# Two halves of a transposed tile in two PSUM pools instead of one

## The chip, the cores and the metric

The kernel runs on one core of a Trainium2 chip. The metric is the device time of one execution in microseconds (us).

## The reference

An adaLN block: modulation vectors come from a condition `c`; then grouped-query attention with cached K and V (32 query heads, 8 KV heads, 2048 queries, 2048 keys, head size 128), then a gMLP block.

```python
mod = (_silu(c) @ w_mod).reshape(c.shape[0], 6, 1, -1)
sa, ca, ga, sb, cb, gb = ...
h = _layernorm(x) * (1 + ca) + sa
x = x + ga * attention(h)          # q = h @ wq; softmax(q k^T / sqrt(128)) v; @ wo
h = _layernorm(x) * (1 + cb) + sb
x = x + gb * gmlp(h)
```

The part that matters is how the first 512 rows of `h` reach the query projection: the kernel normalises a tile of 128 rows, transposes it on PE (TensorE) into PSUM, where this kernel's matmuls and transposes put their results, lets VectorE apply the modulation on the way to SBUF (`hT`), and projects.

## The kernel before

The kernel takes PSUM in tiles of 512 f32 columns, which it calls banks: two score tiles `s_ps` of two banks each, two banks `misc` and two banks `o_ps`. Each name has its own rotation of two; a request gets the bank of the request before last under the same name, and the first write must wait until that earlier tile has been read.

```python
psum = fast.enter_context(tc.tile_pool(name="psum", bufs=2, space=bass.MemoryType.PSUM))
def bank(name):
    return psum.tile([P, 512], FP32, name=name)
def bank2():
    return psum.tile([P, 1024], FP32, name="s_ps")
...
def ln1_turn(j0, n, xns):
    ch, c0 = j0 // CT, (j0 % CT) * P
    hT = hT_of(ch)
    for half in range(2):
        t_ps = bank("misc")[:].bitcast(BF16).rearrange("p (k q) -> p k q", k=2)
        for k in range(2):
            dt = half * 2 + k
            for jj in range(n):
                nc.tensor.transpose(t_ps[:, k, jj * P : (jj + 1) * P],
                                    xns[jj][:, dt * P : (dt + 1) * P], ident[:])   # L827
        for k in range(2):
            dt = half * 2 + k
            dst, src = hT[:, dt, c0 : c0 + n * P], t_ps[:, k, 0 : n * P]
            ln1_mod(dst, src, dt)                                                  # L809, VectorE
```

The query projection takes a `misc` bank, too, and empties it with a VectorE cast:

```python
def qproj(b, heads, c0, n):
    ...
        if dt == 0 and (not one or hh == heads[0]):
            ps[0] = bank("misc")
        ... nc.tensor.matmul(ps[0][...], lhsT=wqs[g][...], rhs=hTs[ch][...])       # L940
            nc.vector.tensor_copy(out=dst, in_=src)                                # L951
```

The attention is cut into units (one query tile and one KV group) of eight slots. "Scores (u, i)" below are the two QK matmuls of unit u, slot i (L973), followed by ScalarE's exponential (L980); "P·V" are the eight matmuls of a slot that use the exponentials of the unit before (L995). In the first unit there is no P·V yet, and the turns and projections of tiles 1 to 3 are put between its scores:

```python
at(0, 3, first_turn)                              # ln1_turn(1, 1), ahead of scores (0,3)
at(0, 6, lambda: ln1_turn(2, 2, first["x2"]))     # tiles 2 and 3, ahead of scores (0,6)
fill[0, 0] = [first_norm]
for i in (1, 2, 3):
    fill[0, i] = [lambda: warm(1)]                # a matmul into o_ps that nobody reads (L781)
next_q = qproj(0, list(range(REP)), P, P)         # projection of tile 1
fill[0, 4], fill[0, 5] = next_q[0:8], next_q[8:16]
rest_q = qproj(0, [0, 1], 2 * P, 2 * P) + qproj(0, [2, 3], 2 * P, 2 * P)
fill[0, 7] = rest_q[0:4]                          # behind scores (0,7)
```

## Time and profile before

| | before |
|---|---|
| time, median of 3 runs | 1321.55 us (1321.16 to 1321.85) |
| span of the profiled run | 1320.0 us |
| PE busy | 1311.8 us (99%) |
| ScalarE busy | 1077.1 us (82%) |
| scores (0,0) start | 10.65 us |
| scores (2,0) start | 27.31 us |
| last PE matmul ends | 1313.68 + 0.84 = 1314.52 us |

In the timeline, a line gives the start and the length of a group of like instructions, the engine (PE is TensorE, DVE VectorE, ACT ScalarE), the source line, the operation, and the tiles out<-in with their shapes; brackets give idle time ahead of it and what ended it. A group's length runs from its first start to its last end, and the ends of matmuls are modelled; so I measure by starts. The prediction shows the groups around the wait in question. Two more lines of the timeline of PE in the kernel before are needed below as marks, the starts of scores (0,0) and (2,0), and one for the end:

```profile
10.65 0.59 PE L973 MATMUL s_ps<-qT,kT 128*128 128x512 bf16 x2
...
27.31 0.60 PE L973 MATMUL s_ps<-qT,kT 128*128 128x512 bf16 x2
...
1313.68 0.84 PE L1357 MATMUL s_ps<-wout_sb,yT 128*128 128x512 bf16 x2
```

From the first of these to the second it is 16.66 us. This distance, taken inside one trace, is free of what happens ahead of the first scores, and it is what the experiments compare.

### The profile page before, as it was taken

How to read it: one execution, taken by the hardware profiler on the slowest of the kernel's cores; microseconds unless marked ns; L12 is line 12 of the kernel's file. 1: busy time of each engine (PE TensorE's matmuls, PEld its weight loads, DVE VectorE, ACT ScalarE, POOL GpSimd, SP SyncE). 2: the span in 40 equal slices, each digit the busy share in tenths (PEclk: the TensorE clock that was granted, in tenths of full speed). 3: DMA queues.
4: the chain of work that ended last, by engine and by line, in shares of the span. 5: the costliest groups of instructions: out<-in, count | busy, mean ns of one | idle time of the engine just before them, and what ended most of it. 6: DMA issues, size and time to landing. Idle time of an engine off the chain costs nothing.

```text
span 1320.0 us, 27930 instructions
## 1 busy us (share of the span) xinstructions
PE 1311.8 (99%) x12359; PEld 857.8 (65%) x12359; DVE 471.7 (36%) x1162; ACT 1077.1 (82%) x1061; POOL 51.8 (4%) x96
## 2 busy tenths in 40 slices
PE   9999999999999999999999999999999999999998
PEld 5666666666666666666666666666666666644445
DVE  5622222222222222222222222222222566794444
ACT  7899999999999999999999999999999999650000
POOL 1201000000000000000000000000000000020000
PEclk9999999999999999999999999999999999999999
DMA  7542121112101111211111211121111112143300
GB/s 180 141 104 47 20 45 37 37 17 50 37 17 37 30 37 37 33 33 38 33 37 13 53 38 33 18 53 22 32 14 21 25 31 33 33 112 84 69 21 26
DMA packets 148944, 58.64 MB, mean 44 GB/s; under 512 B 138480, under 2 KB 144880, under 8 KB 148816
## 3 DMA queue, kind: packets, MB, share of 16 engines
q1 hardware_dynamic: 141792, 37.65, 15.6%
q0 software_dynamic: 4432, 16.91, 4.5%
q8 instruction: 98, 1.61, 0.5%
q10 hardware_dynamic: 2592, 2.23, 0.5%
q14 instruction: 30, 0.25, 0.1%
HBM read 21.89 MB, written 2.10 MB: 18 GB/s over the span
## 4 chain that ended last, share of the span: by engine, by line
PE 99%; DMA 0%; DVE 0%; ACT 0%; SPq 0%; issue 0%; DVEq 0%
PE o_ps L995 35%; PE s_ps L973 34%; PE misc L1027 8%; PE misc L940 8%; PE misc L1336 7%; PE s_ps L1182 2%; PE s_ps L1221 2%; PE o_ps L1357 1%; PE s_ps L1357 1%; DMA wmod_a<-in_w_mod_dram 0%; PE misc L850 0%; ACT pT L980 0%; PE misc L1344 0%; PE o_ps L781 0%; PE misc L827 0%; DVE qT L951 0%
## 5 line engine op out<-in xcount | busy, mean ns | idle before, releaser
L980 ACT ACTIVATE pT<-s_ps 128x1024 bf16<-128x1024 f32 x1024 | 1043.8, 1024 | 82.5 <-PE s_ps L973 7.4
L995 PEld LDWEIGHTS <-pT 128*128 128x128 bf16 x8192 | 548.2, 98 | 241.5
L995 PE MATMUL o_ps<-v,pT 128*128 128x129 bf16 x8192 | 631.7, 220 | 0.0
L973 PE MATMUL s_ps<-qT,kT 128*128 128x512 bf16 x2048 | 609.1, 379 | 0.6 <-ACT pT L980 0.5
L1006 DVE RECIPROCAL rall<-o_ps 128x2 f32<-128x2 f32 x256 | 43.7, 171 | 742.9 <-PE o_ps L995 739.5
L973 PEld LDWEIGHTS <-kT 128*128 128x128 bf16 x2048 | 199.0, 98 | 119.6 <-issue 1.0
L1027 PE MATMUL misc<-wo_g,oT 128*128 128x512 bf16 x512 | 194.2, 379 | 0.0
L940 PE MATMUL misc<-hT,wq_g 128*128 128x512 bf16 (+2 forms) x528 | 190.3, 371 | 0.0
L1007 DVE TENSOR_TENSOR onorm<-o_ps,rall 128x256 bf16<-128x256 f32 x256 | 108.7, 425 | 8.8
L1336 PE MATMUL misc<-wsp,z 128*128 128x512 bf16 (+2 forms) x560 | 100.7, 337 | 0.0
L951 DVE CAST qT<-misc 128x512 bf16<-128x512 f32 x127 | 86.4, 681 | 3.1 <-PE misc L940 3.1
L1336 PEld LDWEIGHTS <-z 128*128 128x128 bf16 x560 | 50.5, 98 | 48.5
L1040 DVE TENSOR_TENSOR xacc<-misc,xacc 128x512 f32<-128x512 f32 x112 | 76.2, 680 | 0.0
L940 PEld LDWEIGHTS <-wq_g 128*128 128x128 bf16 x528 | 50.4, 98 | 0.8
L1027 PEld LDWEIGHTS <-oT 128*128 128x128 bf16 x512 | 50.0, 98 | 0.9
L1351 DVE TENSOR_TENSOR gb<-misc,bsp_bc 128x512 bf16<-128x512 f32 (+1 forms) x28 | 18.4, 658 | 58.5 <-PE misc L1336 58.5
L1182 PE MATMUL s_ps<-win_sb,hT 128*128 128x448 bf16 x128 | 27.0, 353 | 0.0
L1192 ACT ACTIVATE z<-s_ps 128x896 bf16<-128x896 f32 x16 | 14.7, 917 | 14.9 <-PE s_ps L1182 14.9
L1221 PE MATMUL s_ps<-hT,win_sb 128*128 128x512 bf16 x112 | 24.5, 379 | 0.0
L1229 ACT ACTIVATE z1T<-s_ps 128x1024 bf16<-128x1024 f32 x14 | 14.3, 1024 | 10.1 <-PE s_ps L1221 9.1
L692 DVE BATCH_NORM_STATS2 bnst<-x_sb 128x6 f32<-128x512 bf16 x32 | 21.9, 683 | 1.3 <-DMA x_sb<-in_A_x_dram 0.8
L1357 PE MATMUL o_ps<-wout_sb,yT 128*128 128x512 bf16 x84 | 20.1, 379 | 0.0
(86 smaller groups left out, 268.9 us busy)
## 6 DMA issues: line engine op xcount, KB each, us to landing
wq_g<-in_A_wq_dram POOLq DMA_DIRECT2D x7, 512.0 KB, 3.9
v<-in_A_v_cache_dram POOLq DMA_DIRECT2D x7, 512.0 KB, 5.8
wo_g<-in_A_wo_dram POOLq DMA_DIRECT2D x7, 512.0 KB, 4.7
oT<-onorm SPq DMA_TRANSPOSE x128, 2.4
wsp<-in_w_mod_dram POOLq DMA_DIRECT2D x1, 2048.0 KB, 11.8
out_dram<-yout ACTq DMA_DIRECT2D x16, 128.0 KB, 1.7
win_sb<-in_B_w_in_dram POOLq DMA_DIRECT2D x1, 1792.0 KB, 7.7
x_sb<-in_A_x_dram SPq DMA_DIRECT2D x3, 512.0 KB, 5.6
```

Source lines behind the costliest of these rows:

```text
L940: nc.tensor.matmul(ps[0][:, o0 : o0 + n], lhsT=wqs[g][:, dt, hh * DH : (hh + 1) * DH], rhs=hTs[ch][:, dt, c0 : c0 + n], start=(dt == 0), s ...
L951: nc.vector.tensor_copy(out=dst, in_=src)
L973: nc.tensor.matmul(s_ps[:, h * 512 : (h + 1) * 512].rearrange("p (r q) -> p r q", r=REP), lhsT=groups[g]["kT"][:, kt * P : (kt + 1) * P], ...
L980: nc.scalar.activation(out=pTs[u][:, 2 * i : 2 * i + 2, :], in_=s_ps[:].rearrange("p (k q) -> p k q", k=2), func=ACT.Exp, scale=inv_sqrt_dh,)
L995: nc.tensor.matmul(o_ps[:, hh % 2, 0 : DH + 1], lhsT=pTs[u][:, kt, hh * P : (hh + 1) * P], rhs=groups[g]["v1"][:, kt, 0 : DH + 1], start=( ...
L1007: nc.vector.tensor_tensor(out=onorms[u][:, hh - 1 : hh + 1, :], in0=o_ps[:, :, 0:DH], in1=rall[:, c0 : c0 + 2].unsqueeze(2).to_broadcast([ ...
L1027: nc.tensor.matmul(X_ps[:], lhsT=oTs[u][:, hh, :], rhs=groups[g]["wo"][:, hh, :], start=(hh == 0), stop=(hh == REP - 1),)
L1040: nc.vector.tensor_tensor(out=xaccs[j][:], in0=X_ps[:], in1=xaccs[j][:], op=ALU.add)
L1182: nc.tensor.matmul(ps[0][:, hf * 512 : hf * 512 + FC], lhsT=h2Ts[j // CT][:, dt, (j % CT) * P : (j % CT + 1) * P], rhs=win_sb[:, dt, FH + ...
L1221: nc.tensor.matmul(ps[0][:, k * 512 : (k + 1) * 512], lhsT=win_sb[:, dt, f * P : (f + 1) * P], rhs=h2Ts[2 * ch2 + k][:, dt, :], start=(dt ...
L1336: nc.tensor.matmul(g_ps[:, :n], lhsT=z2[:, st, f * P : (f + 1) * P], rhs=wsp[t][:, st, c0 : c0 + n], start=(st == 0), stop=(st == NT - 1 a ...
L1357: nc.tensor.matmul(dst, lhsT=yT[:, f, jj * P : (jj + 1) * P], rhs=wout_sb[:, f, :], start=(f == 0), stop=(f == NFT - 1),)
```

## The change

The second half of a turn is to get its PSUM bank from another pool, so that the two halves don't queue in the rotation of `misc`.

```diff
@@ ln1_turn
         for half in range(2):
-            t_ps = bank("misc")[:].bitcast(BF16).rearrange("p (k q) -> p k q", k=2)
+            t_ps = bank(("misc", "o_ps")[half])[:].bitcast(BF16).rearrange("p (k q) -> p k q", k=2)
             for k in range(2):
```

## The prediction

> **What bounds the kernel now.** I read the page first: the shares of the engines and the chain that ended last.
>
> ```profile
> span 1320.0 us, 27930 instructions
> PE 1311.8 (99%) x12359; PEld 857.8 (65%) x12359; DVE 471.7 (36%) x1162; ACT 1077.1 (82%) x1061; POOL 51.8 (4%) x96
> ...
> PE 99%; DMA 0%; DVE 0%; ACT 0%; SPq 0%; issue 0%; DVEq 0%
> ```
>
> PE is busy for 1311.8 of 1320.0 us and is 99% of the chain of waits. So a microsecond counts only if PE's own stream gets it: PE runs in program order, and what it loses near the start moves everything behind it. The changed lines belong to the first pass over the queries, so the next view is who PE waited for, over the whole run:
>
> ```profile
> PE o_ps L781 <- DVE onorm L763: 1.2, 1, 1.2
> PE misc L827 <- DVE qT L951: 0.6, 1, 0.6
> PE s_ps L973 <- ACT pT L980: 0.5, 2, 0.2
> PE misc L850 <- DMA wmod_a<-in_w_mod_dram: 0.2, 1, 0.2
> ```
>
> The second line is the one that the change is about: L827 is the PE transpose in the changed function, and it waited once, 0.6 us, for a VectorE cast. The timeline of PE around it (columns: start, length, engine, line, operation, tiles, then in brackets idle time and what ended it):
>
> ```profile
> 15.61 0.61 PE L940 MATMUL misc<-hT,wq_g 128*128 128x128 bf16 x8
> 16.05 0.39 PE L827 MATMUL misc<-ident,xn 128*128 128x128 bf16 x4
> 17.00 0.39 PE L827 MATMUL misc<-ident,xn 128*128 128x128 bf16 x4 [0.56 <-DVE qT L951]
> 17.22 1.03 PE L973 MATMUL s_ps<-qT,kT 128*128 128x512 bf16 x4
> 18.08 0.60 PE L940 MATMUL misc<-hT,wq_g 128*128 128x256 bf16 x4
> 18.93 0.59 PE L973 MATMUL s_ps<-qT,kT 128*128 128x512 bf16 x2 [0.24 <-ACT pT L980]
> ```
>
> and of VectorE and ScalarE:
>
> ```profile
> 16.25 0.69 DVE L951 CAST qT<-misc 128x512 bf16<-128x512 f32 x1 [0.51 <-PE misc L940]
> 16.86 1.36 DVE L809 TENSOR_SCALAR hT<-misc,modc 128x256 bf16<-128x256 bf16 x4
> 18.14 0.68 DVE L692 BATCH_NORM_STATS2 bnst<-x_sb 128x6 f32<-128x512 bf16 x1
> ...
> 17.85 1.02 ACT L980 ACTIVATE pT<-s_ps 128x1024 bf16<-128x1024 f32 x1 [0.97 <-PE s_ps L973]
> ```
>
> The misc pool has two buffers, handed out in turn. Counting in the source: the first query projection (L940, ended at about 16.2) holds one, the first half of the turn of tiles 2 and 3 (16.05) gets the other, and the second half needs the first one again, which the cast at 16.25 must empty. The cast ends at 16.94 and PE goes on at 17.00. The score matmuls (L973) stand behind these transposes, so ScalarE's exponential starts at 17.85 after 0.97 us idle.
>
> **What the Trainium skill says.** "Perfetto Trace Analysis", section Matmuls: "Independent matmul groups should rotate through different PSUM banks so the ACT/DVE evacuation of one overlaps the next group's matmuls". The trace shows what happens when the rotation is one bank short: the 0.56 us above. "PSUM — Partial Sum Buffer", section Engine vs sequencer instructions: matmuls start and complete in program order. The trace agrees: the scores at 17.22 follow the held transposes by one issue step. The same page, section PSUM bank collisions raise a hardware error, says that the chip neither arbitrates nor stalls, so that a bank must be guarded by semaphores; hence the wait is the price of the shared bank and can be removed only by another bank. No run here shows a collision.
>
> **The change part by part.** The function is called twice: for one tile (transposes at 13.10) and for two (16.05 and 17.00). Its first half stays in misc, its second half takes o_ps. No instruction is added or removed.
>
> The call at 13.10 had no wait for a bank (all four transposes ran as one group). In o_ps its second half follows a warming matmul, which PE itself wrote and nobody reads. Cost 0.
>
> The second call: transposes issue every (0.39-0.22)/3 = 0.056 us, so four take 0.22 us. Held by nothing, the second half starts at 16.05+0.22 = 16.27 instead of 17.00, **0.73 us earlier** (the 0.56 is shorter because it counts from the modelled end of the last transpose). The o_ps bank it gets was last used by the second half of the first call, whose VectorE reads ended before 15.0. The scores (0,6) start at 16.27+0.22 = 16.49 instead of 17.22. Their own bank is free: ScalarE had finished (0,4) by about 16.0. The next scores need the bank of (0,5), finished at 16.88 (17.85-0.97), so they start at 16.93.
>
> Then something else holds. The projection matmuls at 18.08 need all four modulations (L809). VectorE runs them right after the cast, which is not moved: it waits for the projection that ended at 16.2, not for the transposes. They end at 16.86+1.36 = 18.22. With 0.05 us from VectorE's end to PE's start (16.95 to 17.00 above), the last projection matmul goes at 18.27. Its successor, scores (1,0), follows one step of 0.11 us later ((0.60-0.27)/3, the 0.27 being one such matmul): 18.38 instead of 18.93. ScalarE does not hold it: the exponential (0,6) starts at 17.85-0.73 = 17.12, ends at 18.14, and the bank is seen free at 18.19. So of 0.73 us, **0.55 us** are left: 18.93-18.38.
>
> Does it last? From 18.93 on PE has no listed wait for ScalarE, VectorE or DMA over a tenth of a microsecond. What must arrive by the clock and not by PE's pace has to have over 0.55 us slack. V: issued at 7.80 and 8.42, landing 5.1 to 5.6 us later, at 14; needed at 18.8. The exponential of (0,7), which the scores (1,1) need: at about 18.04 to 19.06, needed at 19.48. The next chunk's hT, which comes by DMA, is the tight one:
>
> ```profile
> 31.09 1.38 DVE L809 TENSOR_SCALAR hT<-hT,modc 128x512 bf16<-128x512 bf16 x4 [2.94 <-DMA hT<-xn]
> 32.38 0.16 DVE L1006 RECIPROCAL rall<-o_ps 128x2 f32<-128x2 f32 x1
> ...
> 32.71 0.59 PE L940 MATMUL misc<-hT,wq_g 128*128 128x512 bf16 x2
> ```
>
> VectorE's statistics start at 18.14, behind the unmoved modulations, and so these four stay at 31.09. PE's pair at 32.71 would come at 32.16 and needs the first two, ready at 31.09+0.41 and about 31.09+0.32+0.41 = 31.82: 0.3 us to spare. ScalarE limits PE for a few slots near 30 us, but it started that run behind PE's scores, so it moves with them.
>
> o_ps hands out two banks more before the main loop, and misc two fewer. Even numbers: the steady rotation keeps its parity. The first P·V sum takes the bank a warming matmul left; the second, four slots of 1.10 us later (about 23), takes the bank that the modulations left at 18.22.
>
> **Sum:** 1321.55 - 0.55 = 1321.0 us.
>
> **The rivals.** First: o_ps becomes the short pool, and P·V waits where the transposes waited. For it: P·V begins only 1.8 us after the transposes. Against: five microseconds of slack for the second sum, and the first gets the other bank. It would give 1321.5 or a little more. Second: the hT transfer, or VectorE behind it, takes the gain back at 32 us: 0.3 us of slack says no, but a shift of that size is possible; then 1321.2 to 1321.5. Third: VectorE isn't late at all and the whole 0.73 us stays. It would need modulations that end before 18.0; they are bound to the cast, so I don't believe it: 1320.8. Fourth: the scatter hides everything. The three runs before spread over 0.69 us, more than the gain.
>
> **Range and chances.** 0.55 us is 0.04% of the time. Every rival stays within 1 us, and the scatter is some 0.35 us to either side. Predicted 1321.0 us, 8 in 10 between 1320.3 and 1321.8. Two per cent are 26 us, out of reach of a change that moves eight transposes: within 2% 0.985, faster 0.01 (something at start that I can't see), slower 0.005.
>
> **What the profile after would show.** The wait of L827 for the cast gone from PE's waits; the eight transposes as one group from 16.05, half of them named o_ps; the exponential near 17.12; modulations still ending at 18.22; PE waiting near 18 for L809, not for ScalarE; scores (1,0) near 18.38; the same 0.55 us shift at 27 us and at 100 us; span near 1319.45. The prediction is wrong if PE waits for an o_ps bank, if VectorE's order around 16 to 18 us changes, if PE waits for hT near 32 us, or if the start (DMA of the modulation weights, on which PE stands until 7.5 us) comes at another time in that run.

## The result, and the profile after

| | before | after |
|---|---|---|
| time, median of 6 runs each | 1321.63 us (1321.16 to 1321.92) | 1321.15 us (1320.97 to 1321.45) |
| ratio of the runs | | 0.9997 (0.9984 to 1.0009) |
| span of the profiled run | 1320.0 us | 1319.7 us |
| scores (0,0) start | 10.65 us | 10.86 us |
| scores (0,0) to (2,0) | 16.66 us | 16.12 us |
| scores (0,0) to the end of the last matmul | 1303.88 us | 1303.33 us |

The ratio stands with its 95% interval. The medians differ by 0.48 us, inside the interval, so the times alone do not settle it. The trace does. First, who PE waited for in the changed kernel:

```profile
PE o_ps L781 <- DVE onorm L763: 1.2, 1, 1.2
PE s_ps L973 <- ACT pT L980: 0.2, 1, 0.2
```

The wait of L827 for the cast is gone, and one of the two waits for ScalarE with it. The timeline of PE at the same place:

```profile
15.82 0.61 PE L940 MATMUL misc<-hT,wq_g 128*128 128x128 bf16 x8
16.26 0.39 PE L827 MATMUL misc<-ident,xn 128*128 128x128 bf16 x4
16.49 0.39 PE L827 MATMUL o_ps<-ident,xn 128*128 128x128 bf16 x4
16.71 1.03 PE L973 MATMUL s_ps<-qT,kT 128*128 128x512 bf16 x4
17.58 1.18 PE L940 MATMUL misc<-hT,wq_g 128*128 128x256 bf16 x4
18.59 0.59 PE L973 MATMUL s_ps<-qT,kT 128*128 128x512 bf16 x2
```

The second half now follows the first after 0.23 us instead of 0.95, and the scores follow at once. But the four projection matmuls of 17.58 need 1.18 us from first start to last end where they needed 0.60 before. There is a gap inside this group, and the timeline of VectorE says what fills it:

```profile
16.46 0.69 DVE L951 CAST qT<-misc 128x512 bf16<-128x512 f32 x1 [0.50 <-PE misc L940]
17.07 0.72 DVE L809 TENSOR_SCALAR hT<-misc,modc 128x256 bf16<-128x256 bf16 x2
17.71 0.72 DVE L809 TENSOR_SCALAR hT<-o_ps,modc 128x256 bf16<-128x256 bf16 x2
```

The modulations end at 18.43, 0.21 us later than before, which is just the 0.21 us by which this run's scores began later: VectorE didn't move. One by one, the four projection matmuls start at 17.58, 17.85, 18.17 and 18.49 us. The last three of them each come 0.05 us after the second, third and fourth modulation ends; unhindered, they would follow one another every 0.11 us. The chain of waits (start, length, what) of the changed kernel runs over these modulations now, where it ran over transposes, scores and an exponential:

```profile
16.46 0.69 DVE qT L951
17.16 1.29 DVE hT L809 x4
18.44 0.04 issue
18.48 0.27 PE misc L940
18.75 0.43 PE s_ps L973 x2
```

And the marks, for start, middle and end. The shift of 0.55 us against the scores' start is the same at 27 us and at 1314 us:

```profile
10.86 0.59 PE L973 MATMUL s_ps<-qT,kT 128*128 128x512 bf16 x2
...
26.98 0.59 PE L973 MATMUL s_ps<-qT,kT 128*128 128x512 bf16 x2
...
1313.35 0.84 PE L1357 MATMUL s_ps<-wout_sb,yT 128*128 128x512 bf16 x2
```

### The profile page after: what moved, and what is told of

It reads as the page before. It is cut to its first block, busy times and chain, and to the rows that moved or that the text cites. A ratio compares the mean times of both kernels' runs of the same rounds, so it can differ in the third digit from the quotient of the medians. Undisturbed runs are those within 1.5% of the kernel's fastest.

```text
span 1319.7 us, 27930 instructions
## 1 busy us (share of the span) xinstructions
PE 1312.4 (99%) x12359; PEld 858.6 (65%) x12359; DVE 470.7 (36%) x1162; ACT 1077.1 (82%) x1061; POOL 51.4 (4%) x96
## 4 chain that ended last, share of the span: by engine, by line
PE 99%; DVE 0%; ACT 0%; issue 0%; DVEq 0%
PE o_ps L995 35%; PE s_ps L973 33%; PE misc L1027 8%; PE misc L940 8%; PE misc L1336 7%; PE s_ps L1182 2%; PE s_ps L1221 2%; PE o_ps L1357 1%; PE o_ps L781 1%; PE s_ps L1357 1%; PE misc L850 0%; DVE hT L809 0%; PE misc L1344 0%; ACT pT L980 0%; DVE tmp L1369 0%; DVE yout L1370 0%
```

## The experiments

My theory has three steps. (1) One wait is removed: that of the second half of the second turn for the bank that the projection of tile 1 holds until its cast. (2) That brings 0.73 us, of which 0.18 are lost to the wait for VectorE's modulations. (3) What is left goes through to the end undiminished. The rivals: each turn in `o_ps` gives a part; the place of the transposes matters and not the shared bank; the loss of 0.18 us is ScalarE's or no wait at all; `o_ps` gets short.

All six kernels gave correct results. Medians are of five runs each; beside them stands the median of nine runs of the kernel before. The first four ran on one chip, the last two on another. Each interval of the ratio includes 1.

| kernel | scores (0,0) start | (0,0) to (1,0) | (0,0) to (2,0) | (0,0) to end of PE | median us | before |
|---|---|---|---|---|---|---|
| before | 10.65 | 8.279 | 16.665 | 1303.879 | 1321.63 | |
| after | 10.86 | 7.732 | 16.119 | 1303.335 | 1321.15 | 1321.63 |
| second call only | 10.71 | 7.732 | 16.119 | 1303.334 | 1321.38 | 1321.77 |
| first call only | 10.27 | 8.279 | 16.665 | 1303.873 | 1321.54 | 1321.77 |
| projection in o_ps | 10.65 | 7.734 | 16.121 | 1303.335 | 1321.06 | 1321.77 |
| P·V into the hole | 10.81 | 7.734 | 15.755 | 1302.984 | 1320.59 | 1321.77 |
| all turns in o_ps | 10.25 | 8.044 | 16.432 | 1303.652 | 1321.45 | 1321.62 |
| scores first | 10.59 | 7.793 | 15.728 | 1302.937 | 1320.69 | 1321.62 |

(For "before" and "after" the medians are those of the result above.) The first column is in us of each trace's own clock, the columns of distances in us from the start of scores (0,0). They come from the starts and ends of single matmuls in the traces. With one trace of each kernel they agree to 0.01 us where the theory says that nothing differs, while the times scatter by over 0.3 us.

### Only the second call

```diff
-            t_ps = bank("misc")[:]...
+            t_ps = bank("o_ps" if half and n == 2 else "misc")[:]...
```

> Only the call for tiles 2 and 3 puts its second half into o_ps; the call for tile 1 stays in misc. My theory (one wait is removed, that of the second half of the second call for the bank which the cast of the projection empties): the whole gain is here. From the start of scores (0,0) to the start of scores (2,0) 16.66 us in the kernel before and 16.11 in the changed one; expected 16.11 +-0.03, no L827 wait for the cast, end about 0.55 us earlier than before. Rival (any second half in o_ps loosens the misc rotation a little, each call gives a part): about half of it, 16.3 to 16.5.

Measured: 16.119 us, just as in the changed kernel, and no wait of L827. The whole gain comes from the second call.

### Only the first call

```diff
-            t_ps = bank("misc")[:]...
+            t_ps = bank("o_ps" if half and n == 1 else "misc")[:]...
```

> Only the call for tile 1 puts its second half into o_ps. The count of banks says that the second half of the later call then still gets the bank of the projection, so my theory: L827 waits 0.56 us for the cast again, scores (0,0) to (2,0) 16.66 +-0.03, time as before (ratio 1.000). Rival (each call gives a part): 16.3 to 16.5.

Measured: 16.665 us as in the kernel before, and the same wait is back in the view of waits of this kernel:

```profile
PE misc L827 <- DVE qT L951: 0.6, 1, 0.6
```

The second half of a turn in `o_ps` is worth nothing in itself. This half of the change does no harm either. (The median time lies 0.23 us under that of the kernel before, with a trace that has the same distances: a measure of the scatter.)

### The projection in o_ps, the turns as before

The wait needs two to share a bank. Here the other one is moved.

```diff
         if dt == 0 and (not one or hh == heads[0]):
-            ps[0] = bank("misc")
+            ps[0] = bank("o_ps" if n == P else "misc")
```

> The turns are as in the kernel before, all in misc; instead the projection of tile 1, whose cast was waited for, takes its bank from o_ps. My theory (the shared bank is the cause, not where the turn lies): the same gain, 16.11 +-0.05 from scores (0,0) to (2,0), VectorE's modulations end at the same distance as in the changed kernel. Rival (the o_ps place of the transposes itself matters): 16.66 or something between.

Measured: 16.121 us. All eight transposes run as one group, and all of them in `misc`:

```profile
16.06 0.61 PE L827 MATMUL misc<-ident,xn 128*128 128x128 bf16 x8
...
16.26 0.69 DVE L951 CAST qT<-o_ps 128x512 bf16<-128x512 f32 x1 [0.51 <-PE o_ps L940]
16.86 1.36 DVE L809 TENSOR_SCALAR hT<-misc,modc 128x256 bf16<-128x256 bf16 x4
```

The modulations end 7.57 us behind the start of scores (0,0), as in the changed kernel and as expected. With all four halves in `misc`, the next request meets the short pool: by the count of banks the last projection takes the bank of the second turn's first half, and it starts 6.99 us behind (0,0) instead of 6.72, 0.06 us after the first two modulations end. This costs nothing here, as its fourth matmul waits for the fourth modulation anyway.

So the cause was the bank shared with the cast, whichever of the two is moved away. The first two rivals are out.

### P·V into the hole

If PE waits for the modulations, PE work put into that gap is free. The first P·V group of unit 0 needs only exponentials that are long done; it is moved from slot (1,0) to slot (0,7), ahead of the projection. The kernel is the changed one otherwise.

```diff
-    fill[0, 7] = rest_q[0:4]
+    fill[0, 7] = [lambda: pv(0, 0)] + rest_q[0:4]
...
-            if 1 <= it <= NU:
+            if 1 <= it <= NU and (it, i) != (1, 0):
                 pv(it - 1, i)
```

> The changed kernel, and the first P.V group of unit 0 (8 matmuls, 0.45 us) moved from behind scores (1,0) to ahead of the last projection of the first pass, where PE waits for VectorE's modulations. My theory (of 0.73 us only 0.55 are kept because PE waits about 0.4 us for the modulations): scores (1,0) stay where they are in the changed kernel, the P.V group costs nothing there, and from then on PE is 0.37 to 0.43 us ahead of the changed kernel; scores (0,0) to (2,0) 15.7 to 15.75, time 0.9 us under before, unless PE now meets the next chunk's hT near 32 us (slack then under 0), which could take back 0.1 to 0.2. Rival (ScalarE holds scores (1,0), not the modulations): scores (1,0) also unchanged but scores (1,1) would wait for ScalarE and 16.0 or more would be seen. Second rival (PE issues that slot back to back with no hole): scores (1,0) 0.45 later, 16.11.

The timeline of PE in this kernel:

```profile
16.66 1.03 PE L973 MATMUL s_ps<-qT,kT 128*128 128x512 bf16 x4
17.53 0.61 PE L995 MATMUL o_ps<-v,pT 128*128 128x129 bf16 x8
17.98 0.73 PE L940 MATMUL misc<-hT,wq_g 128*128 128x256 bf16 x4
18.54 0.59 PE L973 MATMUL s_ps<-qT,kT 128*128 128x512 bf16 x2
18.97 0.38 PE L940 MATMUL misc<-hT,wq_g 128*128 128x256 bf16 x2
19.28 0.59 PE L973 MATMUL s_ps<-qT,kT 128*128 128x512 bf16 x2
```

Scores (1,0) stand at 7.734 us behind (0,0), against 7.732 in the changed kernel: the P·V group of 0.45 us was free. From scores (1,1) on the kernel is ahead of the changed one by 0.36 us, and 0.35 of it reach the end. That is the hole of step 2. That VectorE held scores (1,0), and not ScalarE, the single starts show: the fourth projection matmul comes at 18.44 us, 0.05 us after the fourth modulation ends, and the scores follow it after 0.11 us, while the exponential (0,6), whose bank they take, had ended at 18.31. In size it is a near miss: I had expected 0.37 to 0.43 us. From 18.54 to 19.28 it is 0.74 us, where the PE work between takes 0.65 (0.43 for the scores, 0.22 for two projection matmuls). ScalarE's timeline points to the exponential (0,7), whose bank scores (1,1) take; it ends at 19.23 us, and they start at 19.28:

```profile
18.21 1.02 ACT L980 ACTIVATE pT<-s_ps 128x1024 bf16<-128x1024 f32 x1
```

The last experiment is about these 0.09 us. The hT of the next chunk did not take anything back, as I had thought it might: its modulations started at 30.91 in this run, and the pair of projection matmuls that needs the first two of them started at 31.97 without a listed wait.

### All turns in o_ps

```diff
-            t_ps = bank(("misc", "o_ps")[half])[:]...
+            t_ps = bank("o_ps")[:]...
```

> Both halves of both calls in o_ps. It tests the rival of the prediction that o_ps becomes the short pool. By the count of banks the warming matmul behind the call for tile 1 gets the bank of that call's first half and must wait for VectorE's two modulations of it, to about 14.15 on the clock of the trace before instead of starting at 13.76; PE is then 0.2 to 0.3 us late, the projection, its cast and the modulations with it: scores (0,0) to (2,0) 16.3 to 16.45, half of the gain lost. P.V itself doesn't wait. Rival (a pool's name does not matter, only the count of banks in it): 16.12, as in the changed kernel.

Measured: 16.432 us. `o_ps` becomes the short pool, not for P·V but for the warming matmul, which only wants a bank to write into. The views of waits and of the timeline of PE:

```profile
PE o_ps L781 <- DVE hT L809: 0.5, 1, 0.5
```

```profile
12.70 0.40 PE L827 MATMUL o_ps<-ident,xn 128*128 128x128 bf16 x4
12.93 0.59 PE L973 MATMUL s_ps<-qT,kT 128*128 128x512 bf16 x2
13.99 0.38 PE L781 MATMUL o_ps<-onorm 128*128 128x512 bf16 x1 [0.47 <-DVE hT L809]
...
14.64 0.61 PE L940 MATMUL misc<-hT,wq_g 128*128 128x128 bf16 x8
```

Scores (0,4) come 0.43 us late, and 0.31 us stay from scores (0,5) to the end. The 0.11 us between are another wait of PE, which the delay swallows. In the changed kernel the same eight projection matmuls take longer:

```profile
14.83 0.72 PE L940 MATMUL misc<-hT,wq_g 128*128 128x128 bf16 x8
```

There the fourth of them starts only 0.05 us after the last modulation of tile 1 ends. Here these modulations end at nearly the same distance, 4.20 us behind scores (0,0) against 4.19, but PE comes to the projection later and doesn't wait. Of the gain of 0.545 us, 0.23 are left. The first rival of the prediction is real in this form: had the change put both halves into `o_ps`, over half of its gain would have gone into a new wait for the same engine.

### Scores first

The kernel with the P·V group in the hole, and the second turn behind scores (0,6) instead of ahead of them.

```diff
-    at(0, 6, lambda: ln1_turn(2, 2, first["x2"]))
+    fill[0, 6] = [lambda: ln1_turn(2, 2, first["x2"])]
```

> The kernel with the P.V group in the hole, and the second turn moved behind scores (0,6) instead of ahead of them. ScalarE then goes on to (0,6) without a gap. In the kernel with the P.V group alone scores (1,1) came 0.74 us after (1,0), where the PE work between is 0.65: my theory is that ScalarE holds them by these 0.09 us. Then here: scores (1,0) 0.04 to 0.08 later (the modulations start later behind the transposes), scores (1,1) 0.65 after (1,0), so the end is the same or 0.03 earlier: scores (0,0) to (2,0) 15.72 to 15.76. Rival (the gap of 0.09 is PE's own): 15.80 to 15.84.

The timeline of PE:

```profile
18.39 0.59 PE L973 MATMUL s_ps<-qT,kT 128*128 128x512 bf16 x2
18.82 0.38 PE L940 MATMUL misc<-hT,wq_g 128*128 128x256 bf16 x2
19.04 0.59 PE L973 MATMUL s_ps<-qT,kT 128*128 128x512 bf16 x2
```

Scores (1,1) follow (1,0) after 0.65 us, the PE work alone, so the 0.09 us were ScalarE's. Scores (1,0) come 0.06 us later, as the modulations now start behind later transposes. Together: 15.728 us, 0.03 less than the version before it, and 1302.937 to the end. By the distance this is the best kernel here, 0.94 us ahead of the kernel before. By time it is 1320.69 us and its forerunner 1320.59, each about 1 us under the kernel before; which of the two is faster, the times cannot tell.

## Why the prediction was right

The time, predicted as 1321.0 us, was 1321.15, and the change against the kernel before of the same rounds 0.48 us where 0.55 was predicted. The time by itself says little: the stated range of 1320.3 to 1321.8 us also holds the kernel before (1321.63) and every rival. It is the distances in the traces that bear the mechanism out. Point by point:

- **The wait and its cause.** Right. The bank shared with the cast was the cause, shown by moving either of the two (second call only, projection in o_ps). That the wait can be removed "only by another bank" goes further than the runs: an earlier cast was not tried. The "eight transposes" that the change is said to move are six.
- **0.73 us earlier.** Right: scores (0,6) moved from 6.572 to 5.849 us behind (0,0), by 0.723.
- **0.18 us of it lost to the modulations.** Right: scores (1,0) moved by 0.547 us. That this was VectorE's doing was only argued in the prediction. The starts of the single projection matmuls, 0.05 us behind each modulation, and the P·V group that cost nothing in the hole show it.
- **It lasts.** Right: 0.545 us at 27 us, 0.544 at the end. Of the margins, that of hT held: its modulations began at 31.46 us and the pair that needs them at 32.38. The estimate that they would stay where they were was a little off: measured from the scores' start they came 0.16 us later in this run, with the transfer that they wait for. Over the eight traces this distance went from 19.86 to 20.68 us, and it was shorter for the second call alone than for the kernel before, so it does not follow the change.
- **o_ps is not short.** Right for this change; the experiment with all turns in `o_ps` shows how near it was. The 1.8 us from the transposes to P·V are a slip: they go from the old start of the second half (17.00) to the expected new start of P·V (18.8). In the changed kernel it was 2.5 us (16.49 to 19.02).
- **The marks in the profile.** The exponential was expected near 17.12 and the scores (1,0) near 18.38; with the 0.21 us by which this run's scores started later, 17.33 and 18.59 are due, and 17.34 and 18.59 were measured. The view of waits, however, does not list PE's wait for L809, as was said it would: each of the four matmuls is drawn 0.27 us long where unhindered ones start every 0.11 us, so at most 0.05 us of each wait is left as idle time. Only the length of the group (1.18 us) and the chain of waits show it.
- **Span near 1319.45.** This was missed in the profiled run: 1319.7 (the other five runs of the changed kernel had 1319.2 to 1319.4). The 0.55 us are all there behind the scores' start, but the scores themselves started 0.21 us later. The prediction named the start as something that could differ, and blamed the DMA of the modulation weights. In this run it was not that; two lines of the timeline of PE, of the kernel before and of the changed one, show the warming matmuls ahead of the second group of modulation matmuls:

```profile
5.77 1.46 PE L781 MATMUL o_ps<-onorm 128*128 128x512 bf16 x6
7.46 0.55 PE L850 MATMUL misc<-sc_bf,wmod_a 128*128 128x1 bf16 x16 [0.24 <-DMA wmod_a<-in_w_mod_dram]
```

```profile
5.89 2.08 PE L781 MATMUL o_ps<-onorm 128*128 128x512 bf16 x6
7.81 0.54 PE L850 MATMUL misc<-sc_bf,wmod_a 128*128 128x1 bf16 x16
```

Before, six warming matmuls took 1.46 us, one every 0.215 us, and PE then waited for the weights. In the changed kernel's run the first of them still went at 0.43 us each and the six took 2.08; the weights had arrived meanwhile and were not waited for. The change can't reach this place: it is over five microseconds ahead of the first transposes that it moves (13.43), and the kernel with all turns in `o_ps` had the six in 1.46 us again. The page "TensorE: Matmul & The Clock Gate" of the Trainium skill, section What's actually happening, tells of a clock that starts throttled and is released after a window of activity that is "free-running", so that the moment differs from run to run. These traces agree that it differs: the spacing goes from 0.43 to 0.215 us for 512 columns, and the switch comes between 4.3 and 7.2 us after the span's start. They don't agree with the section on the size, which it gives as 500 ns to either side: here the moments lie up to 2.9 us apart. With the switch, and with the arrival of the weights, the scores' start wandered from 10.25 to 10.86 us over the eight traces, more than the whole effect.

## What to carry to other kernels

When one engine is 99% of the chain, a single wait of it near the start is worth what of it survives to the end: follow the freed time to the next thing that is held, here VectorE's modulations, and look for work to put into the gap that opens there. Count the rotation of each PSUM pool in program order, writers that nobody reads included; a wait for a bank goes away when either of the two tiles that share it moves, and comes back elsewhere when all move to the same pool. For effects below the scatter, measure between two marks inside a trace, behind the part that wanders.

## What the Trainium skill lacked or had wrong

- "Perfetto Trace Analysis", Matmuls, advises to rotate matmul groups through PSUM banks, and the runs agree: the one bank too few cost 0.56 us of idle time. It doesn't say that a wait for a bank can stand with a matmul whose result nobody reads; here a warming matmul waited 0.47 us for a bank.
- "Perfetto Trace Analysis", Optimization Strategy, tells to look for gaps between slices. It doesn't say that a gap can hide under the drawn lengths of matmuls: PE's wait for the modulations is in no list of waits, because each matmul is drawn 0.27 us long, and shows only as 1.18 us instead of 0.60 for a group of four.
- "TensorE: Matmul & The Clock Gate", What's actually happening, lets the moment of the switch vary by 500 ns to either side; the eight traces have it from 4.3 to 7.2 us after the span's start.
- The same page, Seeing it yourself, warns that clock events in a trace have been unreliable. It doesn't say that the profile's row of granted clock can miss the slow start altogether. The row reads full speed in the first slice, and 1.00 in each of the first microseconds, while matmuls of 512 columns went at 0.43 us each until up to 7.1 us. The clock record in the trace has its first entry, full speed, just at the switch (7.19 us in the changed kernel, 5.30 in the kernel before), and none ahead of it.
